# Two banded-attention and feed-forward layers on one core: the operand sums of a seven-product matrix product, moved from GpSimd to VectorE

## The chip, the cores and the metric

The kernel runs on one core of a Trainium2 chip. Each core has five engines that work in parallel, each through its own queue in program order: TensorE (PE; its weight loads are listed as PEld), VectorE (DVE), ScalarE (ACT), GpSimd (POOL) and SyncE (SP), which issues most DMAs. The metric is the time of one execution on the device in microseconds (us). Lower is better.

## The reference

```python
def _attn_ref(q, k, v):                 # 4 batches, 8 heads, 576 tokens, 64 wide; 64-token causal window
    scores = scale * np.matmul(q, k.transpose(0, 1, 3, 2))
    ...
    return np.matmul(attn, v)
def _moe_ref(x, w_in, w_out):           # 2304 tokens, 512 -> 2048 -> 512
    h = x @ w_in
    return (h - np.tanh(h)) @ w_out
def _moe2_ref(x, w_in, w_out):          # the same sizes
    h = x @ w_in
    return (h * (1.0 / (1.0 + np.exp(-1.702 * h)))) @ w_out
```

The output is the second feed-forward layer of the first one of the attention, all float32.

## The kernel before, in words

Every float32 matrix product is made of three products of parts: an operand is split into a high part (a copy to the matmul's rounded type, on ScalarE) and a low part (operand minus high part, on VectorE), and PE computes high by high, high by low and low by high.

The second layer is done for a first block of 256 tokens in the ordinary way and then for 2048 tokens in two **units** of 1024 (u = 0 and 1). A unit uses a scheme in which a 2 by 2 block product takes seven block products in place of eight, at the price of sums of blocks ahead of and behind the products. A unit has two phases.

In the first phase (tiles `m`, helpers `m_open`, `m_first`, `m_more`) the hidden layer is computed for j = 0 to 7. The products' results are combined on VectorE (`u_add`, line 925) into four hidden blocks per j, ScalarE takes the sigmoid of each (`u_act1`, line 933), and the product of block and sigmoid is made on VectorE for one block and on GpSimd for three (`u_act2`, line 937). One sum per j, `T1`, is made on GpSimd here (`u_sub`, line 940).

In the second, the **output phase** (tiles `ob`), seven output products P1, P5, P6, P7, P2, P3, P4 (unit 1: ... P3, P4, P2) run one after the other, each over j = 0 to 7: 56 product tiles, here numbered 0 to 55 in the order in which PE takes them. For a tile, ScalarE writes the high part `gh` of its operand (`o_hi`, line 950), VectorE the low part `gl` (`o_lo`, line 954), and PE does 12 matmuls of 128x256 (`o_prod`, recorded at line 697): the first of `gh` alone, the second of `gl`. `gh` and `gl` have three buffers each, so ScalarE can start the `gh` of tile k when PE has finished tile k - 3. The operand of P5 is T1, of P1, P2 and P3 a hidden block. The operands of P6, P7 and P4 are three more sums of 128x512 float32 per j, in place in the tile `ug`: T2 = C22 - T1 (once the `gl` of P5 has read T1), T3 = T2 - C11 and T4 = C21 - T2. `u_sub` makes them, eight tiles times three, per unit. Nothing else runs on GpSimd in the output phase, after the last hidden blocks of j = 7.

During the output phase of unit 0, VectorE and ScalarE also prepare the inputs of unit 1: two passes (i = 0, 1), in each of which SyncE loads four blocks `xt` (line 871), VectorE combines them (`combine`, line 883) and ScalarE and VectorE split seven results (`u_hi`, line 886, `u_lo`, line 890). The weights of the output products come in 14 chunks `ws` (line 440), four tiles each, into four buffers.

A planner (`Plan`) fixes the order. Each step is a task with its possible engines and an assumed time on each, a due time, what it waits for and which buffers it takes and frees; the planner runs the tasks through a list schedule, by due time where several are ready, and emits the instructions of each engine in the order in which its schedule started them. The sums' tasks are added in `plan_out`, with a due time 8 us ahead of their product tile; that of `gh` and `gl` is 4 us ahead.

Of the kernel before, what the change touches and what calls it, by code (L numbers as in the profile page):

```python
# [16 lines left out]
ALU = mybir.AluOpType  # L17
# [7 lines left out]
class Plan:  # L25
# [11 lines left out]
    def add(self, engs, fn, prio, after=(), acq=(), rel=(), size=0, behind=None):  # L37


        t = dict(engs=engs, fn=fn, prio=prio, acq=acq, rel=rel, size=size, n=len(self.tasks), outs=[], next=[], left=0, at=None, own={})  # L40
        for a in after:
            if a is not None:
                a["outs"].append(t)
                t["left"] += 1
        if behind is not None:
            behind["next"].append(t)
            t["left"] += 1
        self.tasks.append(t)
        return t
# [122 lines left out]
def attn_moe2_kernel(  # L172
# [20 lines left out]
    nc = tc.nc  # L193
# [3 lines left out]
    _, NG, NP, _ = q.shape  # L197
# [51 lines left out]
    add = plan.add  # L249
# [25 lines left out]
    def first(*key):  # L275
        return min(due["h", s] for s in steps if s[0][: len(key)] == key)
# [562 lines left out]
    def keys(names):  # L839
        return tuple("psh" if t == "h" else t for t in names)  # L840
# [76 lines left out]
    def u_val(u, j, o):  # L917
        return ut[u, j][:, PLACE[o]]
# [18 lines left out]
        eng.tensor_tensor(out=u_val(u, j, o), in0=u_sum(u, j, o), in1=ut[u, j, o, "g"], op=ALU.mult)  # L937

    def u_sub(u, j, o, a, b):
        nc.gpsimd.tensor_tensor(out=u_val(u, j, o), in0=u_val(u, j, a), in1=u_val(u, j, b), op=ALU.subtract)  # L940


    PROD = dict(P1=(A11, "C11"), P5=(S1, "T1"), P6=(S2, "T2"), P7=(S3, "T3"), P2=(A12, "C21"), P3=(S4, "C22"), P4=(A22, "T4"))
# [3 lines left out]
    def o_hi(u, n, j):  # L947
        gh, gl = (gp.tile([P, NB], F32R, tag=w, name=w) for w in ("gh", "gl"))
        og[u, n, j] = (gh, gl)
        nc.scalar.activation(gh, u_val(u, j, PROD[n][1]), AF.Copy)  # L950

    def o_lo(u, n, j):
        gh, gl = og[u, n, j]
        nc.vector.tensor_tensor(out=gl, in0=u_val(u, j, PROD[n][1]), in1=gh.bitcast(F32), op=ALU.subtract)  # L954

    def o_prod(u, n, j, es):

        onto = n in ONTO
        if j == 0 and es[0] == 0:
            ob[u, n] = ob[u, ONTO[n]] if onto else [bank(t, "ob") for t in OB[n]]  # L960
        wh, wl = ws_of(("o", u, n, j // 4), j % 4)
        gh, gl = og[u, n, j]
        for e in es:
            c = slice(e * P, (e + 1) * P)
            a = ob[u, n][e // 2][:, e % 2 * HB : (e % 2 + 1) * HB]
            three(a, wh, wl, gh[:, c], gl[:, c], not onto and j == 0 and e % 2 == 0, j == NJ - 1 and e % 2 == 1, swap=True, onto=onto)
# [6 lines left out]
    def o_add(u, o, b):  # L973
        if o == "U":
            z, a, n = ov[u, "U"][:, b], "U", "P6"
        elif o == "W":
            if b == 0:
                ov[u, "W"] = cv.tile([P, 2, NB], F32, tag="raw", name="ow")
            z, a, n = ov[u, "W"][:, b], "U", "P5"
        elif o == "C22":  # L980
            z, a, n = ov[u, "W"][:, b], "W", "P7"
        else:
            z = os_[u, o, b] = st.tile([P, NB], F32, tag="s", name="os")
            a, n = "U", dict(C12="P3", C21="P4")[o]
        nc.vector.tensor_tensor(out=z, in0=ov[u, a][:, b], in1=ob[u, n][b], op=ALU.add)
# [28 lines left out]
    for t, m in masks.items():  # L1014
        nc.gpsimd.memset(m, 0.0)
        for kind, r in zip(t, (slice(0, W), slice(W, P))):
# [5 lines left out]
            for base, cm, step, op in conds:  # L1022
                nc.gpsimd.affine_select(
                    out=m[r], in_=m[r], pattern=[[step, P]], base=base,
# [8 lines left out]
    for i in range(NEARLY):  # L1033
        a = 2 * i
# [14 lines left out]
    for i in range(8):  # L1049
        z = turns[0 if i < 2 else 1 if i < 4 else 2]  # L1050
        d = first(*z) - K["ahead"][i]
# [3 lines left out]
    for bi in range(2, NB1):  # L1055
        t0, n = blocks[1][bi]
        d = first(1, bi)
# [4 lines left out]
    for f in range(KF):  # L1062
        for i in range(2):
            d = due["hp"[i], next(s for s in steps if s[1] == f)]
# [108 lines left out]
    def stream(key, j, a, b, d):  # L1173
        n = len(streams)
        last = list(streams.values())[-1:] or [None]
        if key[0] == "o":
            after, src = wd_done[1, NJ - 1], lambda: wd["out"][:, :, POS[j], a:b]
        else:
            after, src = wd_done[0, j], lambda: wd[j][:, :, a:b]
        after = after + ([last_proj[8 + n]] if n < NS else [])  # L1180
        streams[key] = add({"SP": 0.6}, lambda _: load_ws(key, src()), d - 14, after, acq=("ws",), size=P * (b - a) * NB * 4, behind=last[0])

    for what, s in seq:
        layer, f = s[0][0], s[1]
        if layer == 2 and not wd_done:
            last = None
            for n in range(2 * NJ):
                d = K["wd"][0] + K["wd"][1] * n
# [83 lines left out]
    gate_of = {}  # L1272
    split = {}
    tsum = {}
# [69 lines left out]
    def plan_out(u, n, j, d):  # L1344
        nonlocal prev
        blk, x = PROD[n]
        if j % 4 == 0:
            stream(("o", u, n, j // 4), blk, j, j + 4, d)
        if x in ("T2", "T3", "T4"):
            a, b, w = dict(T2=("C22", "T1", [split[u, "P5", j]]), T3=("T2", "C11", [tsum.get((u, "T2", j)), split[u, "P1", j]]), T4=("C21", "T2", [split.get((u, "P6", j))]))[x]  # L1350
            src_ = tsum[u, x, j] = add({"POOL": 1.25}, lambda _, z=(u, j, x, a, b): u_sub(*z), d - 8, w + [gate_of[u, j][a]] if a in gate_of[u, j] else w)
        else:
            src_ = gate_of[u, j][x]
        first_ = j == 0
        onto = n in ONTO
        h = add({"ACT": 0.54}, lambda _: o_hi(u, n, j), d - 4, [src_] + chain[-4:-3], acq=("gp",))
        lo = split[u, n, j] = add({"DVE": 0.62}, lambda _: o_lo(u, n, j), d - 4, [h])
        slot_free.setdefault((u + 1, j), []).append(lo)
        bk = keys(OB[ONTO.get(n, n)])
        need = [lo, streams["o", u, n, j // 4]]  # L1360
        if first_ and onto:
            need += dict(P2=oo[u, "P1"], P3=oo[u, "W"], P4=oo.get((u, "C22")) if n == "P4" else None)[n]
        final = u == 1 and n == OSEQ[u][-1] and j == NJ - 1
        es = [(0, 1), (2, 3)] if final else [(0, 1, 2, 3)]
        ps = []
        for z in es:
            lastz = z[-1] == 3
            rel = ([("gp", h)] + ([("ws", streams["o", u, n, j // 4])] if j % 4 == 3 else [])) if lastz else []
            p = prev = add({"PE": OC / 4 * len(z)}, lambda _, z=z: o_prod(u, n, j, z), d, [prev] + need, acq=bk if first_ and not onto else (), rel=rel)
            chain.append(p)  # L1370
            ps.append(p)
        if first_ and not onto:
            oo[u, n, "own"] = p
        if j < NJ - 1:
            return
        own = oo[u, ONTO.get(n, n), "own"]

        def sm(o, b, w, **kw):
            return add({"DVE": 0.7}, lambda _: o_add(u, o, b), d + 1.5, w, **kw)

        def put(o, b, w, i=0, k=1, eng="SP", rel=()):
            return add({eng: 0.6}, lambda g: o_store(u, o, b, i, k, g), d - 1, [w], rel=list(rel), size=P * NB * 4 // k)

        if n == "P1":
            c0 = add({"ACT": 0.52}, lambda _: o_one(u, 0), d + 1.5, [p], acq=("raw",))
            oo[u, "P1"] = [c0, add({"ACT": 0.52}, lambda _: o_one(u, 1), d + 1.5, [c0])]
            oo[u, "r1"] = c0
        elif n == "P6":
            us = [sm("U", b, [p, oo[u, "P1"][b]], rel=[(bk[b], own)]) for b in range(2)]
            w0 = sm("W", 0, us, acq=("raw",))  # L1390
            oo[u, "W"] = [w0, sm("W", 1, [w0])]
        elif n == "P7":
            oo[u, "C22"] = [sm("C22", b, [p, oo[u, "W"][b]]) for b in range(2)]
            so = [put("C22", b, oo[u, "C22"][b]) for b in range(2)]
            add({"none": 0.0}, lambda _: None, d, so, rel=[("raw", oo[u, "W"][0])])
        elif n == "P2":
            cuts = 2 if final else 1
            for b in range(2):
                evs = []
                for i in range(cuts):  # L1400
                    engs = {"ACT": 0.52 / cuts, "DVE": 0.62 / cuts}
                    if final:
                        engs = dict([list(engs.items())[i]])
                    evs.append(add(engs, lambda g, a=(u, b, i, cuts): o_evict(*a, g), d + 1 + b * 0.01, [ps[b * (len(ps) - 1)]], acq=("s",)))
                    put("C11", b, evs[-1], i, cuts, "ACT" if final and i else "SP", [("s", evs[-1])])
                add({"none": 0.0}, lambda _: None, d, evs, rel=[(bk[b], own)])
        elif n in ("P3", "P4"):
            o = dict(P3="C12", P4="C21")[n]
            cs_ = [sm(o, b, [p], acq=("s",), rel=[(bk[b], own)]) for b in range(2)]
            for b in range(2):  # L1410
                put(o, b, cs_[b], rel=[("s", cs_[b])])
            if n == "P4":
                add({"none": 0.0}, lambda _: None, d, cs_, rel=[("raw", oo[u, "r1"])])

    for o in order:
        d = due[o]
# [50 lines left out]
```

## Time and profile before

| what | us |
|---|---|
| median of 3 runs (873.61 to 875.83) | 875.72 |
| the profiled execution, own time | 875.41 |
| its span, from the first to the last instruction | 873.6 |
| PE busy in the span | 845.0 |
| DVE busy | 624.3 |
| ACT busy | 433.8 |
| POOL busy | 236.3 |

PE is busy for 97% of the span on average. The averages hide that single stretches have other limits, so the trace is read by stretch: the output phase of unit 0 lies between about 606 and 707 us of the span, that of unit 1 between about 787 and 869 us. The program's order of instructions per engine is known for both kernels; how long something takes or waits comes from the trace alone.

### The profile page before, as it was taken

The page shows a single profiled execution, that of the slowest core. Times are in us where ns is not written, and L with a number is a line of the kernel's source. Part 1 is how long each engine was busy: PE and PEld are TensorE (multiplying, and loading weights), DVE is VectorE, ACT ScalarE, POOL GpSimd, SP SyncE. Part 2 cuts the span into 40 slices and gives each one's busy share as a digit, 9 for nine tenths or more (in the row PEclk, how much of TensorE's full clock was granted, in tenths as well). Part 3 has the DMA queues.
Part 4 walks back from the last instruction along what each step waited for, and adds up shares of the span by engine and source line. Part 5 has one row for each costly group of instructions (what it writes and reads, how often), then busy time and mean ns, then how long its engine had stood idle before and what let it go on. Part 6 is the DMA issues. An engine that isn't in the chain of part 4 may idle for free.

```text
span 873.6 us, 15207 instructions
## 1 busy us (share of the span) xinstructions
PE 845.0 (97%) x5689; PEld 731.5 (84%) x5689; DVE 624.3 (71%) x1002; ACT 433.8 (50%) x997; POOL 236.3 (27%) x219
## 2 busy tenths in 40 slices
PE   8899999999999999999999999999869999999998
PEld 5788888888898878788888898888859988889898
DVE  6999999888789889863234663448997544368974
ACT  7986655547677467652223442325423422334343
POOL 3110000231112223110000002555791015558920
PEclk9999999999999999999999999999978999999999
DMA  9654555777898878833566865456624765665462
GB/s 330 251 174 148 166 147 192 262 226 270 281 298 285 267 259 269 285 129 140 202 210 208 256 202 182 164 184 234 237 95 127 223 205 169 192 231 204 148 212 75
DMA packets 106745, 182.13 MB, mean 208 GB/s; under 512 B 6704, under 2 KB 70192, under 8 KB 106672
## 3 DMA queue, kind: packets, MB, share of 16 engines
q1 hardware_dynamic: 106240, 180.64, 63.1%
q8 instruction: 45, 0.74, 0.3%
q10 hardware_dynamic: 432, 0.52, 0.2%
q14 instruction: 28, 0.23, 0.1%
HBM read 136.05 MB, written 45.09 MB: 207 GB/s over the span
## 4 chain that ended last, share of the span: by engine, by line
PE 76%; DVE 13%; DMA 5%; ACT 4%; issue 2%; SPq 1%; POOL 0%; DVEq 0%; ACTq 0%; POOLq 0%
PE psh L697 21%; PE acc L697 21%; PE m L697 17%; PE ob L697 13%; DVE gl L954 5%; ACT s L591 2%; DMA raw<-in_w_in 2%; PE psa L632 1%; PE psa L559 1%; DVE xu L890 1%; PE psa L615 1%; DVE xt L883 1%; DMA early<-in_q 1%; DMA early<-in_k 1%; DVE s L608 1%
## 5 line engine op out<-in xcount | busy, mean ns | idle before, releaser
L697 PE MATMUL acc<-gh,w 128*128 128x512 f32 (+1 forms) x672 | 198.1, 362 | 0.2 <-DVE w L338 0.2
L697 PE MATMUL psh<-xh,w 128*128 128x512 f32 (+1 forms) x672 | 198.3, 362 | 0.0
L697 PE MATMUL ob<-ws,gh 128*128 128x256 f32 x896 | 168.4, 289 | 0.0
L697 PE MATMUL ob<-ws,gl 128*128 128x256 f32 x448 | 133.1, 297 | 14.5 <-DVE gl L954 14.2
L697 PEld LDWEIGHTS ob<-ws,gh 128*128 128x128 f32 x896 | 144.5, 198 | 0.2
L954 DVE TENSOR_TENSOR gl<-ug,gh 128x512 fp32r<-128x512 f32 x112 | 118.3, 1075 | 35.2 <-ACT gh L950 34.1
L697 PEld LDWEIGHTS psh<-xh,w 128*128 128x128 f32 x672 | 121.5, 189 | 20.9 <-issue 1.5
L697 PEld LDWEIGHTS acc<-gh,w 128*128 128x128 f32 x672 | 121.6, 189 | 20.5 <-issue 0.5
L937 POOL TENSOR_TENSOR ug<-ug,g 128x512 f32<-128x512 f32 x48 | 63.4, 1321 | 275.6 <-ACT g L933 274.5
L697 PE MATMUL acc<-gl,w 128*128 128x512 f32 (+1 forms) x336 | 120.7, 359 | 0.0
L697 PE MATMUL psh<-xl,w 128*128 128x512 f32 (+1 forms) x336 | 120.7, 359 | 0.0
L950 ACT ACTIVATE gh<-ug 128x512 fp32r<-128x512 f32 x112 | 70.2, 629 | 85.8 <-PE ob L697 52.8
L940 POOL TENSOR_TENSOR ug<-ug 128x512 f32<-128x512 f32 x64 | 105.0, 1668 | 8.4 <-DVE gl L954 8.3
L697 PEld LDWEIGHTS ob<-ws,gl 128*128 128x128 f32 x448 | 88.3, 197 | 21.5 <-DVE gl L954 21.3
L723 DVE TENSOR_TENSOR g<-psh,g 128x512 f32<-128x512 f32 (+1 forms) x100 | 57.9, 579 | 67.2 <-ACT g L717 56.5
L380 POOL TENSOR_TENSOR raw<-cw 128x256 f32<-128x256 f32 x32 | 27.4, 855 | 263.2 <-DVE cw L324 191.6
L697 PE MATMUL m<-xu,ws 128*128 128x512 f32 x384 | 92.3, 389 | 0.0
L717 ACT ACTIVATE g<-psh 128x512 f32<-128x512 f32 (+1 forms) x84 | 44.8, 534 | 87.4 <-PE psh L697 87.4
L925 DVE TENSOR_TENSOR ug<-ug,m 128x512 f32<-128x512 f32 x80 | 55.0, 687 | 42.4 <-PE m L697 42.0
L697 PEld LDWEIGHTS m<-xu,ws 128*128 128x128 f32 x384 | 71.9, 188 | 14.9
L731 DVE TENSOR_TENSOR gl<-g,gh 128x512 fp32r<-128x512 f32 (+1 forms) x100 | 63.6, 637 | 20.9 <-ACT gh L727 19.9
L933 ACT ACTIVATE g<-ug 128x512 f32<-128x512 f32 x48 | 30.3, 632 | 89.4 <-DVE ug L925 89.4
(110 smaller groups left out, 1277.2 us busy)
## 6 DMA issues: line engine op xcount, KB each, us to landing
ws<-wdo SPq DMA_DIRECT2D x28, 1024.0 KB, 5.3
ws<-wd SPq DMA_DIRECT2D x24, 1024.0 KB, 6.2
raw<-in_w_in SPq DMA_DIRECT2D x32, 512.0 KB, 4.8
raw<-in_w_out SPq DMA_DIRECT2D x32, 512.0 KB, 4.0
ws<-wd SPq DMA_DIRECT2D x16, 768.0 KB, 7.3
wdo<-wds SPq DMA_DIRECT2D x32, 256.0 KB, 3.5
wd<-wds SPq DMA_DIRECT2D x32, 256.0 KB, 4.0
wo<-wdo SPq DMA_DIRECT2D x8, 1024.0 KB, 5.2
```

The costliest lines, as they stand in the source:

```text
L380: nc.gpsimd.tensor_tensor(out=x[o], in0=x[a], in1=x[b], op=op)
L591: nc.scalar.activation(s[:, h, p, :], x[:, p, :], AF.Exp, bias=nm[:, h, p : p + 1], scale=scale, accum_out=sm[:, h, p : p + 1],)
L697: nc.tensor.matmul(ps, lhsT=a, rhs=b, start=first and i == 0, stop=last and i == 2, skip_group_check=onto)
L717: nc.scalar.activation(g, psh[s], AF.Tanh)
L723: nc.vector.tensor_tensor(out=g, in0=psh[s], in1=g, op=ALU.subtract if s[0][0] == 1 else ALU.mult)
L731: nc.vector.tensor_tensor(out=gl, in0=g, in1=gh.bitcast(F32), op=ALU.subtract)
L925: nc.vector.tensor_tensor(out=u_val(u, j, o), in0=u_val(u, j, a), in1=mb[u, j, n], op=ALU.add)
L933: nc.scalar.activation(g, u_sum(u, j, o), AF.Sigmoid, scale=BETA)
L937: eng.tensor_tensor(out=u_val(u, j, o), in0=u_sum(u, j, o), in1=ut[u, j, o, "g"], op=ALU.mult)
L940: nc.gpsimd.tensor_tensor(out=u_val(u, j, o), in0=u_val(u, j, a), in1=u_val(u, j, b), op=ALU.subtract)
L950: nc.scalar.activation(gh, u_val(u, j, PROD[n][1]), AF.Copy)
L954: nc.vector.tensor_tensor(out=gl, in0=u_val(u, j, PROD[n][1]), in1=gh.bitcast(F32), op=ALU.subtract)
```

## The change: which engine makes T2, T3 and T4

```diff
     def u_sub(u, j, o, a, b):
-        nc.gpsimd.tensor_tensor(out=u_val(u, j, o), in0=u_val(u, j, a), in1=u_val(u, j, b), op=ALU.subtract)
+        (nc.gpsimd if o == "T1" else nc.vector).tensor_tensor(out=u_val(u, j, o), in0=u_val(u, j, a), in1=u_val(u, j, b), op=ALU.subtract)
...
         if x in ("T2", "T3", "T4"):
...
-            src_ = tsum[u, x, j] = add({"POOL": 1.25}, lambda _, z=(u, j, x, a, b): u_sub(*z), d - 8, w + [gate_of[u, j][a]] if a in gate_of[u, j] else w)
+            src_ = tsum[u, x, j] = add({"DVE": 0.62}, lambda _, z=(u, j, x, a, b): u_sub(*z), d - 8, w + [gate_of[u, j][a]] if a in gate_of[u, j] else w)
```

T1 stays on GpSimd. In the two output phases, 48 sums leave GpSimd's queue (24 per unit, the whole of what it does there) and stand in VectorE's; and since the planner assumes 0.62 us for a sum in place of 1.25 us, it also moves other work around them. PE's order stays what it was.

VectorE's queue in the output phase of unit 0, from the place where the two orders part; `gl` is the low part of a product tile (in the second row that of tile 9, P5 of j = 1), `xt` and `t_6719` belong to the inputs of unit 1, `ug<-ug` (line 940) is a sum:

```order
 L890 TENSOR_TENSOR xu<-xt,xu 128x512
 L954 TENSOR_TENSOR gl<-ug,gh 128x512
-L883 TENSOR_TENSOR xt<-xt 128x512
-L954 TENSOR_TENSOR gl<-ug,gh 128x512
-L890 TENSOR_TENSOR t_6719<-xt,t_6718 128x512
-L954 TENSOR_TENSOR gl<-ug,gh 128x512 x4
+L940 TENSOR_TENSOR ug<-ug 128x512 x2
+L954 TENSOR_TENSOR gl<-ug,gh 128x512
+L940 TENSOR_TENSOR ug<-ug 128x512
+L954 TENSOR_TENSOR gl<-ug,gh 128x512
+L940 TENSOR_TENSOR ug<-ug 128x512
+L954 TENSOR_TENSOR gl<-ug,gh 128x512
```

From here on one or two sums stand between any two `gl`, and the last rows of pass i = 0 (`xt`, `t`) come 28 and 31 rows later than this point, behind the `gl` of tiles 21 and 22. From the first sum to the `gl` of tile 41, where the rows for unit 1 end, VectorE's queue holds 74 rows, 24 of them sums; in unit 1 it holds 46 rows from behind the `gl` of tile 9 to that of tile 29, 22 of them sums.

ScalarE's queue at the same place; `ou` is the copy of P1's result, `t_6718` (`t_6933` in the changed kernel) the last high part of pass i = 0, `xh` the first of pass i = 1:

```order
-L971 ACTIVATE ou<-ob 128x512
-L886 ACTIVATE t_6718<-xt 128x512
-L971 ACTIVATE ou<-ob 128x512
+L971 ACTIVATE ou<-ob 128x512 x2
+L950 ACTIVATE gh<-ug 128x512 x12
+L886 ACTIVATE t_6933<-xt 128x512
 L950 ACTIVATE gh<-ug 128x512 x4
 L886 ACTIVATE xh<-xt 128x512
```

The end of pass i = 0 and the start of pass i = 1 move back by twelve `gh`: `xh` now stands behind the `gh` of tile 26 and ahead of that of tile 27, and two more rows of pass i = 1 that wait for loads of their own stand ahead of the `gh` of tiles 31 and 32.

SyncE's queue in the output phase of unit 0; `ws` are chunks of weights of 1 MB, `xt` the loads for unit 1, `out` stores of results:

```order
 L440 DMA ws<-wdo 128x2x1024 x2
 L871 DMA xt<-xs_0_4888 128x512
-L440 DMA ws<-wdo 128x2x1024 x3
+L440 DMA ws<-wdo 128x2x1024 x6
 L871 DMA xt<-xs_0_4888 128x512
 L440 DMA ws<-wdo 128x2x1024
 L871 DMA xt<-xs_0_5525 128x512 x2
 L871 DMA xt<-xs_0_4888 128x512
-L440 DMA ws<-wdo 128x2x1024 x5
+L440 DMA ws<-wdo 128x2x1024 x2
```

The four loads of pass i = 1 move back past three chunks: the first stands behind chunk 8 (the chunk of tiles 32 to 35), the other three behind chunk 9.

## Rows read from the trace of the kernel before

**Rows 1.** The page: busy time, 40 slices, groups (busy, mean ns | idle before).

```profile
PE 845.0 (97%) x5689; PEld 731.5 (84%) x5689; DVE 624.3 (71%) x1002; ACT 433.8 (50%) x997; POOL 236.3 (27%) x219
...
POOL 3110000231112223110000002555791015558920
PEclk9999999999999999999999999999978999999999
...
L954 DVE TENSOR_TENSOR gl<-ug,gh 128x512 fp32r<-128x512 f32 x112 | 118.3, 1075 | 35.2 <-ACT gh L950 34.1
...
L940 POOL TENSOR_TENSOR ug<-ug 128x512 f32<-128x512 f32 x64 | 105.0, 1668 | 8.4 <-DVE gl L954 8.3
```

**Rows 2.** Chain that ended last, in time order: start, duration, what it ran on.

```profile
611.78 0.61 DVE gl L954
...
612.44 4.47 PE ob L697 x35
...
655.56 1.68 DVE gl L954
...
657.28 50.33 PE ob L697 x395
707.62 72.11 PE m L697 x318
...
802.58 20.44 DVE gl L954 x12
```

**Rows 3.** Stretches of the output phases: engines' busy us (instructions), PE clock, DMA.

```profile
612.44:657.28 44.84, 32.25 (x216) 29.62 (x216) 44.64 (x34) 15.53 (x28) 40.61 (x23) 0.88 0.43 154
657.28:707.62 50.34, 50.34 (x396) 50.34 (x397) 30.21 (x44) 20.58 (x33) 1.60 (x1) 0.94 0.63 194
...
786.70:802.30 15.60, 15.60 (x133) 15.60 (x132) 12.12 (x10) 7.90 (x14) 12.52 (x9) 1.00 0.58 208
802.30:828.27 25.97, 25.78 (x184) 22.54 (x182) 25.97 (x21) 9.63 (x16) 25.97 (x16) 1.00 0.48 162
828.27:869.06 40.79, 40.77 (x331) 39.96 (x332) 26.01 (x33) 16.29 (x26) 6.19 (x4) 1.00 0.45 143
```

**Rows 4.** The same view in finer stretches of unit 0.

```profile
650.00:655.00 5.00, 3.85 (x18) 3.43 (x16) 5.00 (x4) 1.67 (x3) 5.00 (x4) 0.50 0.00 0
...
676.00:706.00 30.00, 30.00 (x252) 30.00 (x251) 15.65 (x23) 13.09 (x21) 0.00 (x0) 1.00 0.78 239
```

**Rows 5.** Timeline of POOL, then DVE: start, us, what [idle before].

```profile
616.08 40.61 POOL L940 TENSOR_TENSOR ug<-ug 128x512 f32<-128x512 f32 x23 [4.84 <-DVE gl L954]
...
616.52 0.68 DVE L954 TENSOR_TENSOR gl<-ug,gh 128x512 fp32r<-128x512 f32 x1
617.12 0.68 DVE L883 TENSOR_TENSOR xt<-xt 128x512 f32<-128x512 f32 x1
617.73 0.68 DVE L954 TENSOR_TENSOR gl<-ug,gh 128x512 fp32r<-128x512 f32 x1
618.60 1.51 DVE L890 TENSOR_TENSOR t<-xt,t 128x512 fp32r<-128x512 f32 x1 [0.20 <-ACT t L886]
...
635.29 1.75 DVE L954 TENSOR_TENSOR gl<-ug,gh 128x512 fp32r<-128x512 f32 x1
636.96 1.77 DVE L883 TENSOR_TENSOR xt<-xt 128x512 f32<-128x512 f32 x1
638.65 1.75 DVE L890 TENSOR_TENSOR xu<-xt,xu 128x512 fp32r<-128x512 f32 x1
```

**Rows 6.** Timeline of ScalarE, late in the output phase of unit 0.

```profile
677.41 0.63 ACT L950 ACTIVATE gh<-ug 128x512 fp32r<-128x512 f32 x1 [0.81 <-PE ob L697]
678.85 0.63 ACT L950 ACTIVATE gh<-ug 128x512 fp32r<-128x512 f32 x1 [0.81 <-PE ob L697]
```

**Rows 7.** Transfers on `xt` from issue to landing, then issues between 590 and 710 us.

```profile
DMA to landing us min/median/max: 4.9/6.4/8.4
...
ws<-wdo SPq DMA_DIRECT2D x14, 1024.0 KB, 5.4
```

## The prediction

> **What bounds the kernel now.** I read the page first [rows 1]: PE is busy for 97% of the span, so time can come only from places where PE waits or runs slowly. The row of the granted clock names one such place, two slices near three quarters of the span at 0.9 and 0.7 to 0.8, and GpSimd's row is full in just those slices and once more near the end. Both are output phases. The chain of waits confirms it [rows 2]: through the body of the kernel it runs on PE, but from 611.8 to 657.3 us it runs mostly on VectorE's `gl` and on work for unit 1, and in unit 1 on `gl` again, 20.44 us from 802.58 on. Everywhere else, the first phase of unit 1 (707.62 to 779.7 us) included, PE sets the time.
>
> How much is lost there follows from a count [rows 3, 6]. Late in the phase, when VectorE keeps up, ScalarE starts a `gh` each 1.44 us (677.41, 678.85), each time released by PE: that is a tile of 12 matmuls at full clock, and the 252 matmuls in the 30 us from 676 to 706 agree [rows 4]. In unit 0, PE does 216 + 396 = 612 matmuls from 612.44 to 707.62 us, 51 tiles: 73.4 us at 1.44, but 95.2 us pass. In unit 1 it does 133 + 184 + 331 = 648 from 786.70 to 869.06 us, 54 tiles: 77.8 us, and 82.4 pass. The losses are **21.7 and 4.6 us**, 26.3 in all. A part of the first is the clock: where PE had been idling between tiles, it was granted half (0.50 from 650 to 655 us, the level of 1.2 GHz) [rows 4], and it recovered after the waits ended.
>
> Why VectorE is late is in the timeline [rows 5]. Until 618 us its instructions of 128x512 start 0.60 us apart (616.52, 617.12, 617.73) and each takes 0.68, the last part beside the next one. GpSimd's first sum starts at 616.08, but that changes nothing as long as VectorE's instructions follow one another. Then VectorE waits once, 0.20 us ahead of 618.60, and its next instruction takes 1.51; from there on, beside GpSimd's sums, the same instructions start 1.67 to 1.69 us apart (635.29, 636.96, 638.65), and GpSimd needs 40.61 / 23 = 1.77 us for one sum, its long first one included. In unit 1 twelve `gl` take 20.44 us, 1.70 each [rows 2], beside a GpSimd that is busy for 25.97 of 25.97 us [rows 3]. The two alternate. A tile needs one `gl` per 1.44 us, and at 1.69 VectorE can't deliver; in unit 0 work for unit 1 stands in the same queue, which is why it loses five times as much as unit 1.
>
> **The change part by part.** *Removed:* 48 sums from GpSimd, and with them every GpSimd instruction that runs behind 616 us in unit 0 and behind the last hidden product in unit 1. VectorE's remaining instructions go back to 0.60 us, as they are just before [rows 5]. *Added:* 48 subtractions of 128x512 on VectorE. The nearest row is line 883 at 617.12 us: the same operation, shape, type and place of operands, 0.68 us long and 0.60 to the next start [rows 5]. I take 0.605. From below nothing shortens it, since that is already its spacing with VectorE alone. From above I take 0.68, as if no sum could start under the end of the one before; only few sums follow the instruction they need.
>
> *Does VectorE then keep up?* In unit 0 it was on time until 617 us. From the first sum to the `gl` of tile 41 its queue holds 74 rows: 74 x 0.605 = 44.8 us, and PE takes 32 x 1.44 = 46.1 us for those tiles. It fits, with 3% to spare, and behind tile 41 the queue thins out. Within the stretch no two `gl` have more than two other rows between them, 1.8 us of work to 1.44 of PE, but the next gap has one. The cushion is what a `gl` may be late: its `gh` starts when PE ends the tile three before, so with 0.63 for the `gh` and 0.68 for the `gl` [rows 5, 6] it can be ready some 1.6 us ahead of its use (2.88 + 0.12 - 1.31, less two hand-overs). In unit 1, 46 rows are 27.8 us for 20 tiles of 28.8 us. So both phases should be bound by PE: **21.7 + 4.6 us off**. At 0.68 unit 0 would need 50.3 us, 4.2 over, of which the 1.0 us by which the `gl` of tile 9 is early (done at 617.2, wanted at 612.3 + 4 x 1.44 + 0.12 = 618.2) absorbs some: 3.2 us lost, and unit 1 31.3 us, 2.5 over and 1.6 absorbed: 0.9. That bound is +4.1.
>
> *Moved: the loads for pass i = 1.* Their first stands behind chunk 8, which waits for the end of tile 19. Counting 1.44 per tile from 612.3 us (tile 5), that is 633.9 us; the load is issued at about 634.8, once the last reader of its buffer on VectorE is done too, and lands 6.4 us later (4.9 to 8.4) [rows 7], at 641.2. ScalarE's `xh` waits for it with the `gh` of tile 27 behind it, which could have started at 641.1. At 6.4 us it starts about 0.6 us late, inside the cushion: no cost. At 8.4 us it starts at about 643.8 and PE waits 0.9 us. The other three loads are issued behind chunk 9, at 640.4 to 641.6 us, and land by 648; the `gh` of tiles 31 and 32 stand behind two of them and are about a microsecond late, again inside the cushion; at 8.4 us another 0.4 is lost. I take 0.3 of 0 to 1.3.
>
> *The chunks.* They are freed sooner as PE goes faster, and each stands 12 tiles, 17 us, ahead of its use; they land in 5.4 [rows 7]. Late in the phase PE already runs at 1.44 with these loads at 239 GB/s [rows 4]. No cost. Pass i = 1 ends with the `gl` of about tile 41, some 20 us before PE needs it. T1 and the hidden products of j = 7 stay on GpSimd, so what PE waits just before 612.44 stays, and I don't count it.
>
> **Sum**, against the profiled execution's own 875.41 us (the median of 875.72 is 0.3 us above it): 875.41 - 21.7 - 4.6 + 0.3 = **849.4 us**, 3.0% less.
>
> **Rivals.**
> *VectorE stays just too slow.* If the spacing is 0.68, or some rows don't overlap as they do at 617 us, the +4.1 above applies, 853.2, and with late loads (+1.3) 854.5. For it: the margin in unit 0 is 3%. Against: VectorE's spacing of 0.60 includes rows that change between three kinds of work.
>
> *A sum takes as much from VectorE as it did on GpSimd.* Beside a sum on GpSimd a VectorE instruction comes 1.69 - 0.605 = 1.085 us late [rows 5]. If on VectorE a sum also kept the others back for 1.085, unit 0 would need 50 x 0.605 + 24 x 1.085 = 56.3 us for 46.1 of PE (9.2 lost after the cushion), unit 1 22 x 1.085 + 24 x 0.605 = 38.4 for 28.8 (8.0 lost after it): 849.4 + 17.2 = 866.6. Against: line 883, the same work, alone costs 0.60. The Trainium skill warns of this on the page Perfetto Trace Analysis, "Optimizing Scalar/DVE Operations": moving work between VectorE and GpSimd might not help, since they share a read port. By that rule the time would be this 866.6 or no change; the trace agrees that the two hold each other up (0.60 alone, 1.69 together), but not that it is all one which of them does the sum.
>
> *Slower than before: GpSimd isn't what slows VectorE.* If its 1.69 us came from the traffic of those stretches (loads, ScalarE), the sums would cost 1.69 as well and just lengthen the queue: 74 x 1.69 = 125 us for 46 in unit 0, 78 for 29 in unit 1, some 975 us. Its point of decision: 120 rows that need on average more than (74.9 + 26.3 + 2.6) / 120 = 0.87 us eat the whole gain (74.9 us is 46.1 + 28.8, 2.6 the cushions). Against: the spacing changes within one instruction, when GpSimd gets its turn [rows 5], and late in unit 0 VectorE is busy 15.65 us for 23 instructions, 0.68 each, with transfers at 239 GB/s, more than in the slow stretch (154) [rows 3, 4].
>
> **How the numbers follow.** PE-bound phases as summed: 0.72 (847 to 852 us). VectorE or the loads a little late: 0.18 (852 to 856). The shared cost or another half gain: 0.06 (856 to 873). GpSimd innocent: 0.02. Another 0.02 lie below 847. The range goes from the sum without late loads (849.1), less the 2.2 us over which the runs of one kernel spread, to the upper bounds together (854.5) plus 1: **846.9 to 855.5**. Faster by over 0.3% (about what a measurement of this kernel can tell from no change): 0.96, within 0.3%: 0.02, slower: 0.02.
>
> **What would show it.** GpSimd's line 940 falls from 64 to 16 instructions [rows 1] and VectorE has 48 of it at about 0.68 us; `gl` averages near 0.7 us instead of 1.08 [rows 1]. PE's idle time ahead of `ob` nearly vanishes and its clock has no 7 or 8 near three quarters of the span. The chain shows little of VectorE in the output phases. The span of unit 0's phase shrinks by about 21 us, unit 1's by 4 to 5. I am wrong if `gl` still takes over 1 us there, if ScalarE's `xh` waits for its load long enough that PE idles before tile 27, or if the sums take over 0.7 us and PE waits for `gl` at each tile.

## The result: 875.23 to 848.66 us, and the profile after

| kernel | median, us | runs |
|---|---|---|
| before | 875.23 | 4, 873.61 to 875.83 |
| changed | 848.66 | 4, 847.62 to 849.77 |

The ratio is 0.970 (95% interval 0.9681 to 0.9718): 26.6 us less. Forecast were 849.4 us (range 846.9 to 855.5), 26.0 less than the profiled execution's 875.41. The profiled execution of the changed kernel took 849.77 us, its span is 847.9, 25.7 less than before.

The page of the changed kernel, the lines that answer to [rows 1] and one more group, PE's matmuls on `gl`:

```profile
PE 832.5 (98%) x5689; PEld 725.0 (86%) x5689; DVE 605.0 (71%) x1050; ACT 434.0 (51%) x997; POOL 153.9 (18%) x171
...
POOL 3110000123111332120000000455500015552000
PEclk9999999999999999999999999999999999999999
...
L697 PE MATMUL ob<-ws,gl 128*128 128x256 f32 x448 | 126.9, 283 | 1.6 <-DVE gl L954 1.6
...
L954 DVE TENSOR_TENSOR gl<-ug,gh 128x512 fp32r<-128x512 f32 x112 | 82.4, 737 | 27.9 <-ACT gh L950 26.2
```

VectorE has 48 instructions more and is busy for 19 us less: that alone says that its other instructions had been held up, not loaded. `gl` went from 1075 to 737 ns. PE waits for `gl` 1.6 us in the whole span, and the dip of the granted clock is gone. Line 940 by engine:

```profile
L940 DVE TENSOR_TENSOR ug<-ug x48: 678/684/693, 617.9 to 803.2; 128x512 f32<-128x512 f32 x48
L940 POOL TENSOR_TENSOR ug<-ug x16: 1283/1289/1747, 540.4 to 768.7; 128x512 f32<-128x512 f32 x16
```

The chain that ended last, which answers to [rows 2]: start, duration, what it ran on.

```profile
607.87 1.29 DVE xh L890
609.16 1.71 DVE xu L890
610.86 1.69 DVE xt L883
612.55 0.61 DVE gl L954
...
613.21 73.58 PE ob L697 x611
686.79 72.11 PE m L697 x318
...
765.88 77.05 PE ob L697 x642
```

Both output phases are now one unbroken run of PE. Unit 0's takes 73.58 us where 95.2 passed, unit 1's 77.05 where 82.36 passed: 21.6 and 5.3 us, 26.9 together. The span shrank by 25.7 only, because the phase of unit 0 began 0.77 us later in this execution (613.21 against 612.44) and what follows unit 1's phase took 0.4 longer (4.97 against 4.54). What is left of the waits are the rows ahead of 613.21: beside GpSimd's last hidden products and the last T1, VectorE's rows still last 1.7 us.

VectorE's timeline where the sums begin, as in [rows 5]:

```profile
617.29 0.68 DVE L954 TENSOR_TENSOR gl<-ug,gh 128x512 fp32r<-128x512 f32 x1
617.89 1.28 DVE L940 TENSOR_TENSOR ug<-ug 128x512 f32<-128x512 f32 x2
619.10 0.68 DVE L954 TENSOR_TENSOR gl<-ug,gh 128x512 fp32r<-128x512 f32 x1
619.70 0.68 DVE L940 TENSOR_TENSOR ug<-ug 128x512 f32<-128x512 f32 x1
```

A sum takes 0.60 us of VectorE's time, and the rows around it too. The stretches of both phases, as in [rows 3] (busy us and instructions of PE, PEld, DVE, ACT and POOL, then granted clock, DMA share, GB/s):

```profile
613.21:656.00 42.79, 42.79 (x356) 42.79 (x357) 42.16 (x70) 22.48 (x38) 0.00 (x0) 1.00 0.65 225
656.00:686.79 30.79, 30.79 (x258) 30.79 (x257) 20.57 (x32) 14.26 (x23) 0.00 (x0) 1.00 0.75 227
765.88:842.93 77.05, 77.05 (x644) 77.05 (x644) 56.76 (x86) 33.80 (x55) 4.29 (x3) 1.00 0.52 173
```

In the first stretch PE is busy throughout, at full clock, and VectorE is busy for 42.16 of 42.79 us: it keeps up, with next to nothing to spare.

### The profile page after: what moved, and what is told of

Same layout as the page of the kernel before. It is cut to its first block, busy times and chain, and to the rows that moved or that the text cites. A ratio compares the mean times of both kernels' runs of the same rounds, so it can differ in the third digit from the quotient of the medians.

```text
span 847.9 us, 15194 instructions
## 1 busy us (share of the span) xinstructions
PE 832.5 (98%) x5689; PEld 725.0 (86%) x5689; DVE 605.0 (71%) x1050; ACT 434.0 (51%) x997; POOL 153.9 (18%) x171
## 4 chain that ended last, share of the span: by engine, by line
PE 87%; DVE 5%; ACT 5%; DMA 1%; issue 1%; SPq 0%; DVEq 0%; POOL 0%; ACTq 0%; POOLq 0%
PE psh L697 23%; PE acc L697 22%; PE ob L697 18%; PE m L697 18%; ACT s L591 3%; PE psa L632 2%; PE psa L559 2%; PE psa L615 1%; DMA raw<-in_w_in 1%; DMA xt<-xs 0%; PE wps L1011 0%; DVE s L608 0%; DVE xu L890 0%; DVE xt L883 0%; DVE g L723 0%
## 5 line engine op out<-in xcount | busy, mean ns | idle before, releaser
L697 PE MATMUL ob<-ws,gh 128*128 128x256 f32 x896 | 161.9, 283 | 0.0
L697 PEld LDWEIGHTS ob<-ws,gh 128*128 128x128 f32 x896 | 140.0, 192 | 0.2
L697 PE MATMUL ob<-ws,gl 128*128 128x256 f32 x448 | 126.9, 283 | 1.6 <-DVE gl L954 1.6
L954 DVE TENSOR_TENSOR gl<-ug,gh 128x512 fp32r<-128x512 f32 x112 | 82.4, 737 | 27.9 <-ACT gh L950 26.2
L697 PEld LDWEIGHTS ob<-ws,gl 128*128 128x128 f32 x448 | 86.0, 192 | 2.0 <-DVE gl L954 1.8
L727 ACT ACTIVATE gh<-g 128x512 fp32r<-128x512 f32 (+1 forms) x100 | 54.3, 544 | 37.1 <-DVE g L723 36.8
```

Of the source, the lines that this page charges most:

```text
L697: nc.tensor.matmul(ps, lhsT=a, rhs=b, start=first and i == 0, stop=last and i == 2, skip_group_check=onto)
L727: nc.scalar.activation(gh, g, AF.Copy)
```

## The experiments

The theory: GpSimd's sums held VectorE to one row per 1.69 us. Rivals: the traffic of the stretch did it; it is the sums as a load on VectorE's or GpSimd's queue that count, not whom they hold up; or the planner's new order did it, not the engine. Each kernel differs from the changed one by the edit shown. All were measured beside the kernel before (875.23 us for the first four experiments, 874.69 for the last four, 7 runs each).

### The order alone

```diff
     def u_sub(u, j, o, a, b):
-        (nc.gpsimd if o == "T1" else nc.vector).tensor_tensor(...)
+        nc.gpsimd.tensor_tensor(...)
```

> The changed kernel's program order on every engine, but the 48 sums stay on GpSimd. My theory (GpSimd's sums hold VectorE's instructions at 1.69 us): in unit 0 VectorE now has fewer rows per tile while the sums last, since the work for unit 1 stands later: 25 rows from the low part of tile 10 to tile 28, 25 x 1.69 = 42 us for 19 tiles of 27.4, so about 13 us lost in place of 21.7; unit 1 loses its 4.6 as before. About 866 us (860 to 873). Rival, the new order gives the gain: 848.7. Rival, the order gives nothing: 875.

Measured: 861.56 us (860.61 to 862.53), ratio 0.9845 (0.9829 to 0.9862). The sums are back on GpSimd, and still half of the gain is there. Its stretches: unit 0 while GpSimd makes its sums, the rest of that phase, unit 1:

```profile
615.66:656.95 41.29, 37.89 (x281) 34.38 (x281) 40.58 (x30) 17.41 (x30) 41.29 (x24) 1.00 0.51 180
656.95:693.69 36.74, 36.74 (x306) 36.54 (x305) 26.53 (x42) 17.45 (x28) 0.00 (x0) 1.00 0.67 208
772.77:855.02 82.25, 82.17 (x645) 78.13 (x644) 64.00 (x62) 33.82 (x55) 44.50 (x27) 1.00 0.47 161
```

While GpSimd makes its 24 sums, one in 1.72 us, VectorE gets 30 rows done, 23 of them `gl` and 3 for unit 1. The kernel before got 27 rows done beside 23 sums (40.61 us), but only 15 were `gl`, and 12 were for unit 1. So the two take turns in both, and the order decides who gets VectorE's few turns. The new order gives them to PE's next tiles and leaves unit 1's inputs for later; unit 0's phase then takes 81.7 us (from 612.02), 8.1 over 73.6. My forecast for it was 13, since I had counted every row of VectorE at 1.69. Four were not slowed, those that read PSUM (line 985, below); at 1.085 us each they are 4.3 us of the difference. In this run the granted clock stays at 1.00 although PE waits (busy for 37.89 of 41.29 us), where it fell before; so what the clock had cost unit 0 before, some 2.8 us (worked out below), belongs to what the order gives here.

```profile
647.22 0.68 DVE L985 TENSOR_TENSOR ou<-ou,ob 128x512 f32<-128x512 f32 x1
647.82 1.18 DVE L954 TENSOR_TENSOR gl<-ug,gh 128x512 fp32r<-128x512 f32 x1
648.92 0.67 DVE L985 TENSOR_TENSOR ou<-ou,ob 128x512 f32<-128x512 f32 x1
649.52 1.18 DVE L954 TENSOR_TENSOR gl<-ug,gh 128x512 fp32r<-128x512 f32 x1
```

A row with one operand in PSUM (`ob`) takes 0.67 us beside GpSimd's sum, and the pair of rows 1.70, a single turn. In unit 1, where nearly nothing else stands in VectorE's queue, the order changes nothing: 82.25 us against 82.36 before.

### The engine alone

```diff
-            src_ = tsum[u, x, j] = add({"DVE": 0.62}, ...
+            src_ = tsum[u, x, j] = add({"POOL": 1.25}, ...
```

The sums are on VectorE, in the order that the planner makes for GpSimd.

> The sums on VectorE, but planned as on GpSimd (1.25 us on its queue), so that the order of everything else stays what it was before the change. My theory (rows at 0.605 us): work for unit 1 and sums stand close together; at tile 29 VectorE's queue is 60 rows behind tile 9, 36.3 us for 28.8 of PE, 7.5 over and 1.0 absorbed: 6.5 us lost in unit 0, nothing in unit 1. About 855 us (853 to 857). Rival, only the engine counts: 848.7. Rival, the order is what counts: 870 or more.

Measured: 857.2 us (856.25 to 857.31), ratio 0.9793 (0.9778 to 0.9808), 0.2 us above the range that I had given. Its stretches of unit 0, then unit 1:

```profile
613.06:654.71 41.65, 37.63 (x288) 35.20 (x288) 41.62 (x70) 20.00 (x36) 0.00 (x0) 1.00 0.53 191
654.71:693.73 39.02, 39.02 (x324) 39.02 (x325) 21.47 (x32) 16.08 (x26) 0.00 (x0) 1.00 0.70 219
772.82:811.11 38.29, 37.59 (x314) 37.38 (x313) 34.50 (x53) 18.02 (x30) 4.30 (x3) 1.00 0.54 194
811.11:850.86 39.75, 39.75 (x331) 39.75 (x332) 22.66 (x34) 15.78 (x25) 0.00 (x0) 1.00 0.46 147
```

VectorE does 70 rows in 41.65 us, 0.60 each, and GpSimd none: nothing holds it up any more. It is simply full, with only 25 `gl` among the 70, since the work for unit 1 stands early; PE gets 24 tiles in place of 29. Unit 0's phase takes 80.7 us (7.1 over), unit 1's 78.0 (1.0 over), where 6.5 and nothing were expected; in unit 1 the chain that ended last runs on VectorE's rows from 803.75 to 811.11 us. The gains of the order alone (13.7 us) and of the engine alone (18.0) add up to more than the 26.6 of both, because each undoes part of the same loss in unit 0.

### Unit 0 alone

```diff
-        (nc.gpsimd if o == "T1" else nc.vector).tensor_tensor(...)
+        (nc.gpsimd if o == "T1" or u == 1 else nc.vector).tensor_tensor(...)
...
-            ... add({"DVE": 0.62}, ...
+            ... add({"POOL": 1.25} if u else {"DVE": 0.62}, ...
```

> The change in unit 0 alone; unit 1's 24 sums stay on GpSimd, planned as such. My theory: unit 0 gains 21.7 and unit 1 nothing, 848.7 + 4.6 = 853.3 us (852 to 855). Rival, the two units share the gain in proportion to their sums (13 each): 862.

Measured: 854.42 us (852.63 to 855.46), ratio 0.9762 (0.9741 to 0.9782). Unit 1 is worth 5.8 us, unit 0 the other 20.8. Its chain shows both: unit 0 as in the changed kernel, unit 1 with single tiles of 1.70:

```profile
612.84 73.57 PE ob L697 x611
...
765.50 15.99 PE ob L697 x133
781.49 1.70 PE ob L697 x12
```

### GpSimd busy with multiplications that nobody needs

```diff
+    spare = [None]
     def u_sub(u, j, o, a, b):
...
+        if o == "T2" and j == 0:
+            spare[0] = gp.tile([P, NB], F32, tag="g", name="spare", bufs=2)
+            nc.gpsimd.memset(spare[0], 1.0)
+        if o != "T1":
+            nc.gpsimd.tensor_tensor(out=spare[0], in0=spare[0], in1=spare[0], op=ALU.mult)
```

48 instructions on GpSimd that no result waits for; VectorE's order is that of the changed kernel.

> The changed kernel, and in each output phase GpSimd does 24 multiplications of 128x512 in a buffer of its own, for which nobody waits (and one memset ahead of them). My theory: each of them makes one VectorE instruction 1.085 us late, 24 x 1.085 = 26 us per unit, less the room of 1 to 2 us: about 900 us (892 to 908), with VectorE's rows at 1.69 us and the clock falling as before. Rival, GpSimd doesn't slow VectorE: 848.7.

Measured: 888.21 us (888.02 to 888.7), ratio 1.015 (1.0133 to 1.0168): 39.5 us more than the changed kernel, and below the range that I had given. GpSimd's timeline, then VectorE's during and after it (lines 961 and 942 of this kernel are `gl` and the sums):

```profile
612.57 34.78 POOL L947 TENSOR_TENSOR spare<-spare 128x512 f32<-128x512 f32 x24
```

```profile
627.57 1.52 DVE L961 TENSOR_TENSOR gl<-ug,gh 128x512 fp32r<-128x512 f32 x1
629.01 1.52 DVE L942 TENSOR_TENSOR ug<-ug 128x512 f32<-128x512 f32 x1
...
647.82 0.68 DVE L961 TENSOR_TENSOR gl<-ug,gh 128x512 fp32r<-128x512 f32 x1
648.42 0.68 DVE L942 TENSOR_TENSOR ug<-ug 128x512 f32<-128x512 f32 x1
```

Idle work on GpSimd makes VectorE's rows come 1.45 us apart, and when it ends at 647.35 they are back at 0.60 with the next row. So it is GpSimd that slows VectorE, and not the traffic. The size was off because the turn is 1.45 us with these multiplications of one buffer by itself, not the 1.69 of the sums that I used: 48 x (1.45 - 0.605) = 40.6 us, against 39.5 measured. That they lie so close is partly luck, since two terms that this product leaves out go against each other: VectorE's room of some 2 us (below) takes off, and the granted clock, 0.96 from 823.91 us to the end of unit 1's phase, adds about as much (461 matmuls in an unbroken 57.66 us; at 0.12 each 55.3).

### GpSimd busy with writes only

```diff
         if o != "T1":
-            nc.gpsimd.tensor_tensor(out=spare[0], in0=spare[0], in1=spare[0], op=ALU.mult)
+            nc.gpsimd.memset(spare[0], 1.0)
```

(The edit is to the kernel above.)

> As the kernel with idle sums, but GpSimd only writes: 25 memsets of 128x512 float32 per output phase in a buffer of its own, which nobody reads. If it is GpSimd's reading of SBUF that excludes VectorE's instructions with two SBUF inputs: 848.7 us as the changed kernel, VectorE's rows at 0.60. If any GpSimd access does: VectorE's rows beside them come late by the length of a memset, and the time is 855 to 900 by that length.

Measured: 848.53 us (847.91 to 850.15), ratio 0.9698 (0.9684 to 0.9713): the time of the changed kernel. Timeline of GpSimd, then of VectorE in the same microseconds:

```profile
610.80 13.96 POOL L947 MEMSET spare<- 128x512 f32 x24
```

```profile
617.37 0.68 DVE L961 TENSOR_TENSOR gl<-ug,gh 128x512 fp32r<-128x512 f32 x1
617.98 0.67 DVE L942 TENSOR_TENSOR ug<-ug 128x512 f32<-128x512 f32 x1
```

For these 14 us GpSimd writes without a pause, 0.58 us for each write of 128x512, and VectorE keeps its 0.60. So a GpSimd that is busy writing does not slow VectorE here; one that reads its operands from SBUF does. The Trainium skill says this on the page SBUF — State Buffer, "Who interferes with whom": a VectorE instruction with two SBUF inputs contends with a GpSimd instruction that reads SBUF, not with one that only writes it, and one with at most one SBUF input does not contend outside the two-port modes. This case agrees in all three parts: 1.69 and 1.45 us for two inputs beside a reader, 0.60 beside a writer, 0.67 for `ou` with its PSUM input.

### How much room VectorE has left: sums twice, T2 twice

```diff
         (nc.gpsimd if o == "T1" else nc.vector).tensor_tensor(...)
+        if o != "T1":        # in the second kernel: if o == "T2"
+            nc.vector.tensor_tensor(out=u_val(u, j, o), in0=u_val(u, j, o), in1=u_val(u, j, o), op=ALU.max)
```

The maximum of a tile with itself leaves it unchanged: 48 rows more on VectorE in the first kernel, 16 in the second. (In the second expectation, 4.0 and 2.8 us are what is left of 5.0 and 4.4 after the cushions of 1.0 and 1.6.)

> The changed kernel with each of the 48 sums followed on VectorE by an instruction of the same shape that leaves its result as it is (the maximum of the sum with itself). My theory (0.605 us a row, PE 1.44 a tile): at the worst place unit 0 is 14.3 us over and unit 1 13.3; with 1.0 and 1.6 absorbed 25 us lost, 874 us (870 to 882, as each extra row waits for the one before it and the clock may fall). Rival, VectorE has room for more: 848.7 to 855.

> The same for T2 alone: 16 extra rows in all. My theory: 5.0 us over at tile 16 in unit 0 and 4.4 in unit 1, less the cushions 4.0 + 2.8, 855.5 us (853 to 859, with waits between the pairs). Rival, there is room for eight more rows a unit: 848.7.

Measured: 879.84 us (878.88 to 881.51), ratio 1.006 (1.0043 to 1.0076), and 858.13 us (857.46 to 859.26), ratio 0.9806 (0.9792 to 0.9821). Both lie above the point forecast, inside its range. The first kernel's VectorE (line 940 the sums, 942 the added rows):

```profile
615.80 0.68 DVE L940 TENSOR_TENSOR ug<-ug 128x512 f32<-128x512 f32 x1
616.51 0.69 DVE L942 TENSOR_TENSOR ug<-ug 128x512 f32<-128x512 f32 x1
617.12 0.68 DVE L940 TENSOR_TENSOR ug<-ug 128x512 f32<-128x512 f32 x1
617.84 0.69 DVE L942 TENSOR_TENSOR ug<-ug 128x512 f32<-128x512 f32 x1
```

The added row needs the result of the row right before it and starts 0.71 or 0.72 us after it, 0.11 later than a row that doesn't (0.605). 48 x 0.11 = 5.3 us on the forecast of 874 gives 879.3, 16 x 0.11 = 1.8 on 855.5 gives 857.3, both within 0.9 us of the medians. The 16 rows in the second kernel are 11.4 us of work at 0.71 and cost 9.5: the room that VectorE has in the changed kernel is some 2 us over both phases.

### T1 on VectorE too

```diff
-        (nc.gpsimd if o == "T1" else nc.vector).tensor_tensor(...)
+        nc.vector.tensor_tensor(...)
...
-        t1 = add({"POOL": 1.25}, ...
+        t1 = add({"DVE": 0.62}, ...
```

> The changed kernel with T1 on VectorE as well, so that GpSimd keeps only the three products with the sigmoid per j. My theory: the one wait left in unit 0's output phase (1.6 us ahead of the second matmul of tile 5, behind VectorE rows at 1.7 us beside GpSimd's T1 and products) gets shorter by about 1 us: 847.7 us (847 to 849). Rival, VectorE in the first phase now comes late for PE, as its T1 waits for GpSimd's products and later rows stand behind it: 850 to 853.

Measured: 848.34 us (847.74 to 849.87), ratio 0.9696 (0.9681 to 0.971): 0.3 us under the changed kernel, which such runs don't tell from nothing. Its group of PE's matmuls on `gl`:

```profile
L697 PE MATMUL ob<-ws,gl 128*128 128x256 f32 x448 | 126.9, 283 | 1.2 <-DVE gl L954 1.2
```

PE's last wait fell from 1.6 to 1.2 us, where about 1 us less was expected, and the first phase of unit 1, bound by PE, neither gained nor lost (72.11 us in both chains). No version beat the changed kernel measurably.

## Why the prediction was right, by its own steps

- *The losses, 21.7 and 4.6 us.* Unit 0 gave back 21.6. The prediction named the clock as a part of this, without a size. Behind the last wait PE was busy for all of 50.34 us [rows 3] at a granted clock of 0.94, with 396 matmuls, which take 47.5 us at 0.12 each [rows 4]: so some 2.8 of the 21.6 us were the clock (an estimate), and the rest passed while VectorE held PE up. Unit 1's term was mis-sized: 5.3. Its 648 matmuls were added up over three adjoining stretches [rows 3], and a matmul that straddles an edge counts in both; the chain of after has 642, that is 53.5 tiles, 77.0 us at 1.44 in place of 77.8.
- *A sum costs VectorE 0.605.* The rows start 0.60 apart and last 0.684. The bound of 0.68 did not occur; what does occur, 0.71 for a row that needs the one right before it, the sums' order almost never meets.
- *VectorE keeps up by 3%.* It does: its 74 rows run from 617.89 us to the `gl` of tile 41, which starts at 663.21, at the pace of PE. It is busy for 42.16 of the first 42.79 us, and the two doubling experiments show how little is left.
- *The price of the new order.* I counted its queue as it stands, 74 rows to the `gl` of tile 41, but spoke of the gain as that of the engine; none of the rivals was the order. The runs show that at the old order the engine alone gives 18.0 of the 26.6 us: with the work for unit 1 early, VectorE is too slow for PE even at 0.60. The order alone gives 13.7. So the forecast held for the change as a whole, engine and order together, not for the engine by itself.
- *Late loads, 0.3 us.* They came out at nothing. SyncE issued them 0.9 us later than forecast (634.8 and from 640.4 on):

```profile
635.71 0.43 SPq L871 DMA_DIRECT2D xt<-xs  x1
...
641.31 1.76 SPq L871 DMA_DIRECT2D xt<-xs  x3
```

They landed in 5.4 to 6.4 us. ScalarE's `xh` waited for the first, `gh` started right behind it, and the next `gh` again waited for PE (ScalarE's timeline):

```profile
642.12 0.63 ACT L886 ACTIVATE xh<-xt 128x512 fp32r<-128x512 f32 x1 [0.74 <-DMA xt<-xs]
642.66 0.61 ACT L950 ACTIVATE gh<-ug 128x512 fp32r<-128x512 f32 x1
643.63 0.63 ACT L950 ACTIVATE gh<-ug 128x512 fp32r<-128x512 f32 x1 [0.35 <-PE ob L697]
```

So the cushion of three buffers held, as the prediction said it would.

- *The rivals.* VectorE just too slow: refuted by PE's unbroken 73.58 and 77.05 us. Moved work that costs VectorE the same 1.085 us: refuted by the 0.60 above. That rival stood beside the page Perfetto Trace Analysis, "Optimizing Scalar/DVE Operations", of the Trainium skill: what it warns of does not happen here, 3.0% less time, since a sum holds VectorE for 0.60 us when VectorE makes it and for 1.085 when GpSimd does. GpSimd innocent: refuted by the idle multiplications (1.45 beside them, 0.60 behind) and the writes (0.60).

One wait in the old trace stays open: GpSimd's first sum at 616.08 did not slow VectorE until VectorE's first pause at 618.4 [rows 5]. In the order-only run it was the same, a first sum at 615.66 and rows 0.60 apart until the pause ahead of 617.25. But beside the idle multiplications, which began at 612.57, VectorE's rows came 1.45 apart from 613.10 on, without a pause. Which of the two gets its turn first, and when, no run here separates.

## What to carry to other kernels

Where two engines hold each other up, compare not how long an operation lasts on each but how much time of the engine that the path waits for it takes away: here 0.60 us when VectorE does the sum itself, 1.085 when GpSimd does it beside it. Look, too, at what stands in the queue of the engine that is held up; with GpSimd's sums left in place, an order that puts the rows that PE waits for first gave 13.7 of the 26.6 us. And before adding to an engine that is 70% busy over the span, count its rows in the stretch where it must keep up: here 16 more rows cost 9.5 us.

## What the runs showed of the hardware that was not expected

- The turn that VectorE gets beside GpSimd depends on GpSimd's instruction: 1.69 us beside subtractions of two tiles, 1.45 beside a multiplication of a tile by itself, though both read two operands of 128x512. It isn't the multiplication as such: at 607.89 us of the trace before, a multiplication of two tiles (line 937) lasted 1.66 us, and VectorE's row beside it held the next one back for 1.71, as the sums do. That points to the one tile read twice, which no run tests by itself. GpSimd's row, then VectorE's:

```profile
607.89 1.66 POOL L937 TENSOR_TENSOR ug<-ug,g 128x512 f32<-128x512 f32 x1
608.31 1.78 DVE L890 TENSOR_TENSOR xu<-xt,xu 128x512 fp32r<-128x512 f32 x1
610.02 1.76 DVE L883 TENSOR_TENSOR xt<-xt 128x512 f32<-128x512 f32 x1
```

- A VectorE row of 128x512 float32 that uses the result of the row just before it starts 0.71 us after it, the rows around it, which do not, 0.60 to 0.61.
- VectorE's rows with an operand in PSUM pass beside GpSimd's sums in 0.67 us, inside the turn of their neighbour.
